# Second-half weights of eight mode groups read in 8 KB runs, and an uneven split by partitions moved to a later transfer

## The chip, the cores and the metric

The kernel runs on one core of a Trainium2 chip. That core has a matrix engine (TensorE, PE in the profile, with its weight loads as PEld), a vector engine (DVE), a scalar engine (ACT), GpSimd (POOL), a sync engine (SP), and sixteen DMA engines that all queues share. The metric is the device time of one execution in microseconds. Three unprofiled runs of the kernel before took 431.48, 431.50 and 431.73 us, so the median is 431.5 us. Lower is better.

## The reference

Sliding-window causal attention (batch 8, 8 heads, 576 positions, head dimension 64, window 64) is followed by a spectral mixing layer:

```
attn = softmax(q k^T / 8, masked to 0 <= i - j < 64) v        # 8 x 8 x 576 x 64
x    = attn, heads side by side                               # 8 x 576 x 512
X    = rfft(x, axis=1)[:, :64]                                # 64 modes
Yr   = Xr w_r - Xi w_i ;  Yi = Xr w_i + Xi w_r                # w_r, w_i: 64 x 512 x 512, one matrix a mode
y    = irfft(Y, 576)
u    = x + y
out  = u + max(u w_ch, 0)                                     # w_ch: 512 x 512
```

All inputs are float32 in HBM. The two weight tensors of the modes are 64 MB each, and each element is used once, for the eight batches; q, k and v are 9.4 MB each.

## The kernel before

**Work.** First comes the attention, in two halves of heads, then the 64 modes, then the inverse transform with the last product and the output. The weights of the modes are read all the while, from the first microseconds on. Every load of weights and of q, k and v is issued on POOL's queue, because it turns float32 into bfloat16 on its way, and the queue is served in the order of issue. A load of 1 MB as the profile counts it is 1 MB of bfloat16 in SBUF and 2 MB of float32 read.

**Modes in groups.** Modes are taken in groups of four, 16 groups in all, through the list `steps`. Groups 0 to 9 (`EARLY = 10`) are worked in two halves of the contracted channels: the first halves (`hb = 0`) during the attention, from heads 0 to 3; the second halves (`hb = 1`) after it. One step of a half takes two loads, one of `moe_w_r` (`ri = 0`) and one of `moe_w_i` (`ri = 1`), each with four modes. In it a partition holds two rows of 512 channels of each mode, so one contiguous run in HBM is 4 KB and lands as 2 KB. The last six groups come whole, two modes a load, with four rows on a partition: runs of 8 KB that land as 4 KB. In the text a load is named by its step, so (15, 0) is the `ri = 0` load of step 15, the second half of group 5.

**Products.** `mode_half` (L201) does the four modes of a half step: two products of 128 rows for each mode, every mode in its own 32 columns of the PE array, 8 matmuls of 512 columns a load. `mode_pair` (L215) does the whole modes, 16 matmuls of 256 columns a load. The left-hand side is the transform X with Xr, Xi and -Xi laid side by side: `XQ[0]` for heads 0 to 3, `XQ[1]` for heads 4 to 7, where partition p has channels 2p and 2p + 1. `whole_modes` (L675) re-lays the X of the last 24 modes so that partition p has channels 4p to 4p + 3 (`XA`, in the memory of `XQ[0]`), with eight small matmuls by a strided identity, four ACT copies and DVE negations; it stands before the third step of the second halves.

**Loading.** `load_weights` (L151) issues loads as buffers come free: eight of 1 MB in two rings (`ringA` with 3, `ringB` with 5). The last six groups use `ringA` alone. A buffer is free when PE has consumed it. POOL's DMAs take eight semaphores in turn, so that at most eight of them are under way and the ninth waits for the first to land.

**The uneven split.** One load, (15, 0) (`SPLIT`, L105), is cut: three modes in one DMA of 128 partitions, and the fourth mode in six DMAs over 87, 2, 4, 6, 5 and 24 partitions (`SHARES`, L106).

**Around it.** The loop at L1067 runs the second halves and the whole modes. For each load it calls the products, then `load_weights`, then a share of the other work (`advance`): products of x with `w_ch` (`x_jobs`, L655), which need the load of `w_ch` issued at L1096, and, near the end, the inverse transform of the modes that are done. After the last load come the last modes' products, the remaining tiles and the output.

```
            elif (at, ri) == SPLIT:
                parts = [[(p, p + 1, p + 2), (p + 3,)]]
...
            open_to = "a" if at >= 2 * EARLY else "aby" if at < EARLY + 2 else "ab"
...
            for size in SHARES if nload == UNEVEN and len(ps) == 1 else (128,):
```

Of the kernel before, what the change touches and what calls it, by code (L numbers as in the profile page):

```python
# [13 lines left out]
ALU = mybir.AluOpType  # L14
# [12 lines left out]
def kernel(  # L27
# [10 lines left out]
    nc = tc.nc  # L38
    B, H, S, D = q.shape
    NM = moe_w_r.shape[0]  # L40
    DM = moe_w_ch.shape[0]
# [7 lines left out]
    HALF = DM // 2  # L49
    NJ = 2  # L50
    NW = DM // 128
# [16 lines left out]
    ident_bf = consts.tile([128, 128], BF16, name="ident_bf")  # L68
# [14 lines left out]
    XQ = {0: xpool.tile([128, 3 * NJ + 2, B, NM], BF16, name="XQ0")}  # L83
# [14 lines left out]
    steps = [(grp, 0) for grp in range(EARLY)] + [(grp, 1) for grp in range(EARLY)]  # L98
# [2 lines left out]
    NMF = 4 * (NGRP - EARLY)  # L101
    XA = XA[:, 0:(3 * NW + 2) * B * NMF].rearrange("p (s b m) -> p s b m", b=B, m=NMF)
    steps += [(grp, hb) for grp in (*range(EARLY, LAST), *range(LAST + 2, NGRP), LAST, LAST + 1) for hb in range(2)]
    ONES = 3, 0
    SPLIT = EARLY + 5, 0  # L105
    SHARES = 87, 2, 4, 6, 5, 24  # L106
    wlist = []
    for at, (grp, hb) in enumerate(steps):
        for ri in range(2):
            p = 4 * grp  # L110
            if (at, ri) == ONES:
                parts = [[(p, p + 1)], [(p + 2,)], [(p + 3,)]]
            elif grp >= EARLY:
                p += 2 * hb
                parts = [[(p, p + 1)]]
            elif (at, ri) == SPLIT:
                parts = [[(p, p + 1, p + 2), (p + 3,)]]
# [5 lines left out]
    UNEVEN = wstart[SPLIT[0]] + SPLIT[1]  # L123
    assert sum(SHARES) == 128

    def lend(t, g=2):
        t = t.rearrange("p (t g j e) -> p t g j e", g=g, j=NJ, e=DM)
# [23 lines left out]
    def load_weights(n):  # L151
        nonlocal nload
        while nload < len(wlist):
            at, parts, hb, ri = wlist[nload]
            if 2 * n <= sum(len(ps) for ps in parts):
                return
            if nload in lent:
                w = lent[nload]
            else:
                open_to = "a" if at >= 2 * EARLY else "aby" if at < EARLY + 2 else "ab"  # L160
                h = min(open_to, key=lambda h: held[h][0] if len(held[h]) == room[h] else -1)
                if len(held[h]) == room[h]:
                    if held[h][0] not in spent:
                        return
                    held[h].pop(0)
                held[h].append(nload)
                if h == "y":
                    w = lentY
                else:
                    w = {"a": ringA, "b": ringB}[h].tile([128, 4, NJ, DM], BF16, name="wi" if ri else "wr", tag="wt")  # L170
            src = moe_w_i if ri else moe_w_r
            if at >= 2 * EARLY:
                w = w.rearrange("p (m h) j e -> p m (h j) e", m=2)
                p = parts[0][0]
                for m, k, lo, hi in ((0, 1, 0, NW), (1, 1, 0, NJ), (1, 1, NJ, NW)) if nload == len(wlist) - 1 else ((0, 2, 0, NW),):
                    nc.gpsimd.dma_start(  # L176
                        out=w[:, m:m + k, lo:hi],
                        in_=src[p + m:p + m + k].rearrange("m (p j) e -> p m j e", j=NW)[:, :, lo:hi])
# [3 lines left out]
                continue  # L182
            to = 0
            for ps in parts:
                row = 0
                for size in SHARES if nload == UNEVEN and len(ps) == 1 else (128,):
                    of = src[ps[0]:ps[-1] + 1, HALF * hb:HALF * hb + HALF, :].rearrange("g (p j) e -> p g j e", j=NJ)
                    nc.gpsimd.dma_start(out=w[row:row + size, to:to + len(ps)], in_=of[row:row + size])  # L188
                    row += size
# [8 lines left out]
    def spend(at, ri):  # L198
        spent.update(i for i, w in enumerate(wlist) if w[0] == at and w[3] == ri)

    def mode_half(psm, at, ri):  # L201
        grp, hb = steps[at]
        pairs = range(4 * grp, 4 * grp + 4)
        for j in range(NJ):
            for p in pairs:
                g = p % 4
                nc.tensor.matmul(out=psm[32 * g:32 * g + 32, :],  # L207
                                 lhsT=XQ[hb].rearrange("k s b m -> k (s b) m")[:, (3 * j + 1 - ri) * B:(3 * j + 5 - ri) * B, p],
                                 rhs=wtiles[p, hb, ri][:, j], start=(ri == 0 and j == 0), stop=(ri == 1 and j == NJ - 1),
                                 tile_position=(0, 32 * g))  # L210
        for p in pairs:
            wtiles.pop((p, hb, ri))
        spend(at, ri)

    def mode_pair(psm, at, ri):  # L215
# [17 lines left out]
    with tc.manual_schedule():  # L233
# [177 lines left out]
        at = scratch[:, 3 * NTC * NM:3 * NTC * NM + NTC]  # L411
# [6 lines left out]
        for nm in ("k", "q", "v"):  # L418
# [17 lines left out]
                         op0=ALU.max, op1=ALU.min)  # L436
# [82 lines left out]
        for it in range(-3, NU + 3):  # L519
# [23 lines left out]
            g = starts.get(it + 2)  # L543
# [26 lines left out]
        trigX = zpool.tile([128, 128], BF16, name="trigX")  # L570
        trigXr = zpool.tile([128, 128], FP32R, name="trigXr")
        XL = zpool.tile([128, 3 * NW + 2, B, 8], BF16, name="XL")
        trpool = pool("trpool", bufs=2, reuse_waits="tile")

        banks = {"m": pool("ps_mc", bufs=2, space=PSUM, reuse_waits="tile"),
# [5 lines left out]
        def bank(h, shape=(128, DM), dtype=FP32, name=None):  # L581
            return banks[h].tile(list(shape), dtype, name=name or "ps" + h, tag="bank")
# [482 lines left out]
        spread = []  # L1065
        n0, n1 = 2 * EARLY, 4 * (NGRP - EARLY)
        for i, (grp, hb) in enumerate(steps[EARLY:]):  # L1067
            if i == 2:
                whole_modes()
            if i == EARLY:  # L1070
                while tables:
                    tables.pop(0)()
                close(stmp2, yp, ringB)
                Zall = pool("zall", side="right").tile([2 * NM, B, DM], FP32R, name="Zall")
                x_jobs(pool("xp1", side="right", reuse_waits="tile"), NX0, NT)
                utpool = pool("utpool", side="right", reuse_waits="tile")
                nc.vector.memset(YT[:, :, :, rows], 0.0)
                homes.append(utpool.tile([128, 2, DM], FP32, name="utx"))
                spread = spread_steps(homes[0])
                given = 0  # L1080
            psm = bank("m")
            for ri in range(2):
                if half == n0 + n1 - 2:
                    while jobs or pend:
                        advance()
                (mode_half if grp < EARLY else mode_pair)(psm, EARLY + i, ri)
                load_weights(len(wlist))
                while ready:
                    ready.pop(0)()
# [101 lines left out]
```

## Time and profile before

| | |
|---|---|
| median of three runs | 431.5 us (431.48 to 431.73) |
| the profiled execution | 432.55 us |
| its span, first to last instruction | 430.4 us |
| PE busy | 327.7 us (76%) |
| DVE busy | 239.4 us (56%) |
| ACT busy | 182.4 us (42%) |
| POOL busy | 106.9 us (25%) |
| DMA | 93.28 MB as landed, 217 GB/s on average; 163.58 MB read from HBM |

The span is divided into engines' busy time, and the DMA share is the mean busy share of the sixteen DMA engines. Packets overlap a little, so the share can stand over 1. The chain that ended last follows the work back from the end of the execution; a piece of it named DMA is the time from the issue of a load to its landing, queueing included. The trace also holds, for each load, the sixteen times at which a DMA engine told that its part had landed; the last of them releases whoever waits.

### The profile page before, as it was taken

To read this page: it belongs to the slowest core of one execution; us is meant where nothing else is said; L and a number is where in the kernel's file an instruction comes from. 1 tells how busy PE (TensorE), PEld (TensorE's weight loads), DVE (VectorE), ACT (ScalarE), POOL (GpSimd) and SP (SyncE) were. 2 spreads that over 40 slices of the span, in tenths; PEclk is the share of its full clock that TensorE was granted. 3 is DMA by queue.
4 is the path that set the end of the run, shared out by engine and by line. 5 is a ranking of instruction groups with operands and counts; after the bars stand their busy time and mean duration, and the time that the engine had idled before them with its cause. 6 is when DMAs were issued, how large, how long until landed. Compare 5 with 4: busy or idle time off the path is not lost.

```text
span 430.4 us, 11427 instructions
## 1 busy us (share of the span) xinstructions
PE 327.7 (76%) x4962; PEld 219.4 (51%) x5006; DVE 239.4 (56%) x509; ACT 182.4 (42%) x330; POOL 106.9 (25%) x159
## 2 busy tenths in 40 slices
PE   6888899888999989975317246576586758989994
PEld 3666767576667666751104123344454545545552
DVE  8688787867676776876103212132222224874995
ACT  6665667565666657532201101124122213433663
POOL 8321223222132131112015100011111111120894
PEclk9999999999999999996556865579988889999999
DMA  8999999999999999999999999999999999996698
GB/s 205 212 211 212 211 212 211 211 212 211 212 211 211 212 213 210 213 211 213 211 257 173 211 212 212 215 214 215 215 215 214 214 214 214 215 215 123 226 368 305
DMA packets 40978, 93.28 MB, mean 217 GB/s; under 512 B 2688, under 2 KB 2944, under 8 KB 40928
## 3 DMA queue, kind: packets, MB, share of 16 engines
q0 software_dynamic: 35216, 81.80, 98.7%
q1 hardware_dynamic: 5568, 10.62, 6.8%
q8 instruction: 39, 0.64, 0.5%
q10 hardware_dynamic: 144, 0.13, 0.1%
q14 instruction: 11, 0.09, 0.1%
HBM read 163.58 MB, written 9.44 MB: 402 GB/s over the span
## 4 chain that ended last, share of the span: by engine, by line
DMA 55%; PE 25%; issue 11%; DVE 3%; POOL 3%; ACT 2%; DVEq 0%; POOLq 0%
DMA wi<-in_moe_w_i_dram 24%; DMA wr<-in_moe_w_r_dram 15%; DMA rawk<-in_k_dram 8%; DMA wch<-in_moe_w_ch_dram 8%; PE tr L269 4%; PE s L316 3%; PE s L328 2%; PE pt L336 2%; PE vb L281 2%; PE psm L207 2%; PE psz L655 2%; PE psm L225 1%; PE o L356 1%; PE s L308 1%; DMA vd<-in_k_dram 1%
## 5 line engine op out<-in xcount | busy, mean ns | idle before, releaser
L655 PE MATMUL psz<-wch,tr 128*128 128x512 f32 x176 | 62.8, 488 | 12.4 <-DMA wch<-in_moe_w_ch_dram 11.4
L876 DVE CAST xw<-psz 128x512 fp32r<-128x512 f32 x36 | 24.9, 692 | 80.1 <-PE psz L655 79.4
L320 DVE TENSOR_REDUCE mx<-s 128x4 fp32r<-128x512 f32 x72 | 49.6, 689 | 24.0 <-PE s L316 23.7
L623 ACT CAST tr<-ptx 128x512 fp32r<-128x512 bf16 x36 | 21.2, 590 | 90.3 <-PE ptx L648 90.3
L655 PEld LDWEIGHTS psz<-wch,tr 128*128 128x128 f32 x176 | 36.7, 232 | 20.2 <-issue 11.8
L330 ACT ACTIVATE p<-s 128x512 bf16<-128x512 f32 x72 | 39.7, 603 | 13.2 <-PE s L328 13.2
L207 PEld LDWEIGHTS <-XQ 128*32 128x32 bf16 x320 | 13.0, 175 | 43.7 <-issue 25.5
L316 PE MATMUL s<-kT,qT 64*64 64x128 bf16 (+1 forms) x576 | 29.1, 221 | 6.7 <-issue 6.7
L273 ACT COPY kT<-tr 128x576 bf16<-128x576 bf16 x32 | 23.2, 724 | 23.2 <-PE tr L269 23.2
L207 PE MATMUL psm<-wi,XQ 128*32 128x512 bf16 x144 | 15.1, 498 | 18.4 <-DMA wi<-in_moe_w_i_dram 18.4
L339 DVE COPY pts<-pt 128x1024 bf16<-128x1024 bf16 (+1 forms) x40 | 25.2, 630 | 5.3 <-PE pt L336 3.8
L273 ACT COPY qT<-tr 128x576 bf16<-128x576 bf16 x32 | 23.3, 728 | 9.6 <-PE tr L269 9.4
L316 PEld LDWEIGHTS <-qT 64*64 64x64 bf16 x576 | 18.0, 107 | 17.7 <-issue 17.2
L176 POOL DMA_DIRECT2D wr<-in_moe_w_r_dram x12 | 8.4, 697 | 74.4 <-PE psm L225 38.0
L328 PE MATMUL s<-mx,ident_r 128*128 128x512 f32 x72 | 26.2, 437 | 0.0
L695 DVE TENSOR_TENSOR stg<-psm,Yfour 128x512 bf16<-128x512 f32 x10 | 6.9, 691 | 34.3 <-PE psm L207 31.6
L207 PE MATMUL psm<-wr,XQ 128*32 128x512 bf16 x120 | 12.8, 509 | 16.0 <-DMA wr<-in_moe_w_r_dram 15.4
L273 ACT COPY vT<-tr 128x576 bf16<-128x576 bf16 x32 | 23.3, 727 | 4.0 <-PE tr L269 4.0
L225 PEld LDWEIGHTS <-XQ 128*32 128x32 bf16 x256 | 9.5, 151 | 29.1 <-issue 26.8
L188 POOL DMA_DIRECT2D wi<-in_moe_w_i_dram x18 | 13.6, 754 | 42.7 <-PE psm L207 31.9
L336 PE MATMUL pt<-ident_bf,p 128*128 128x128 bf16 x288 | 23.2, 220 | 0.7 <-issue 0.5
L256 POOL DMA_DIRECT2D rawk<-in_k_dram x15 | 8.1, 539 | 60.5 <-PE tr L269 49.5
(260 smaller groups left out, 678.6 us busy)
## 6 DMA issues: line engine op xcount, KB each, us to landing
wi<-in_moe_w_i_dram POOLq DMA_DIRECT2D x29, 1024.0 KB, 18.0
wr<-in_moe_w_r_dram POOLq DMA_DIRECT2D x26, 1024.0 KB, 17.3
out_dram<-ut SPq DMA_DIRECT2D x29, 256.0 KB, 2.7
rawv<-in_v_dram POOLq DMA_DIRECT2D x16, 288.0 KB, 16.4
rawk<-in_k_dram POOLq DMA_DIRECT2D x15, 288.0 KB, 15.2
rawq<-in_q_dram POOLq DMA_DIRECT2D x15, 288.0 KB, 15.1
x_sb<-in_moe_w_r_dram POOLq DMA_DIRECT2D x2, 1024.0 KB, 16.3
out_dram<-utx SPq DMA_DIRECT2D x6, 256.0 KB, 2.4
```

Of the source, the lines that this page charges most:

```text
L207: nc.tensor.matmul(out=psm[32 * g:32 * g + 32, :], lhsT=XQ[hb].rearrange("k s b m -> k (s b) m")[:, (3 * j + 1 - ri) * B:(3 * j + 5 - ri) ...
L269: nc.tensor.transpose(out=pt[ro, j, :], in_=raw[ro, TH * half + j, :], identity=ident_bf[ro, ro])
L273: nc.scalar.copy(out=to, in_=pt.rearrange("p j n -> p n j"))
L316: nc.tensor.matmul(out=s[ro, t, lo:128], lhsT=lq, rhs=kT[ro, 64 * n - 64 + lo:64 * n + 64], start=False, stop=True, skip_group_check=True)
L320: nc.vector.tensor_reduce(out=mx, in_=s, axis=AX.X, op=ALU.max, negate=True)
L328: nc.tensor.matmul(out=s, lhsT=ident_r, rhs=mx.unsqueeze(2).to_broadcast([128, 4, 128]), start=False, stop=True, skip_group_check=True)
L330: nc.scalar.activation(out=p[:, 4 * c2:4 * c2 + 4, :], in_=s, func=ACT_F.Exp, scale=EX_SCALE)
L336: nc.tensor.transpose(out=pt[:, t, :], in_=st[u]["p"][:, t, :], identity=ident_bf)
L339: nc.vector.tensor_copy(out=ps[:, 0:nt, :], in_=pt[:, 0:nt, :])
L623: nc.scalar.copy(out=tr, in_=pt)
L655: nc.tensor.matmul(out=pz, lhsT=tr[:, c, :], rhs=wch[:, c, :], start=(c == 0), stop=(c == NDCH - 1))
L876: nc.vector.tensor_copy(out=XW[i], in_=multiply(tr))
```

## The change

The second halves of groups 2 to 9 (`WIDE = 2`: steps 12 to 19, sixteen loads) are laid differently. Two modes share the 128 partitions: partition 2p takes four rows of the one mode, and partition 2p + 1 four rows of the other, in runs of 8 KB that land as 4 KB. One load is two DMAs of 512 KB, one for each pair of modes. A new function, `wide_modes`, makes an X to match (`XE`, in the memory of `XQ[1]`): for each of the two modes of a pair, X with zeros on the partitions of the other. `mode_wide` does 16 matmuls of 512 columns a load where `mode_half` does 8. `whole_modes` moves one step earlier, to the second step of the second halves, and its copy of `XL` moves behind `wide_modes`, which first uses the memory of `XL` for its strided identity.

Load (15, 0) is no longer split. In its place the first load of the last six groups, (20, 0), is cut into six DMAs: 25 partitions of both modes, 11 of both, then 80 of each mode by itself, then 12 of each.

```diff
+    XE = XQ[1].rearrange("p s b m -> p (s b m)")
+    WIDE = 2
+    NE = 2 * (EARLY - WIDE)
+    SHARES = 25, 11, 80, 12
+    XE = XE[:, 0:2 * (3 * NW + 2) * B * NE].rearrange("p (h s b m) -> p h s b m", h=2, b=B, m=NE)
-    SPLIT = EARLY + 5, 0
-    SHARES = 87, 2, 4, 6, 5, 24
...
             if at >= 2 * EARLY:
...
+                if nload == wstart[2 * EARLY]:
+                    row = 0
+                    for i, size in enumerate(SHARES):
+                        for m in [slice(0, 2)] if i < 2 else [slice(0, 1), slice(1, 2)]:
+                            nc.gpsimd.dma_start(
+                                out=w[row:row + size, m],
+                                in_=src[p:p + 2][m].rearrange("m (p j) e -> p m j e", j=NW)[row:row + size])
+                        row += size
...
+            if at >= EARLY + WIDE:
+                w = w.rearrange("p (q h) j e -> p q (h j e)", q=2)
+                for i in range(2):
+                    p = parts[0][2 * i]
+                    nc.gpsimd.dma_start(
+                        out=w[:, i], in_=src[p:p + 2, HALF:DM, :].rearrange("h (p j) e -> p h (j e)", j=NW))
+                    wtiles[p, hb, ri] = w[:, i].rearrange("p (j e) -> p j e", j=NW)
...
-                for size in SHARES if nload == UNEVEN and len(ps) == 1 else (128,):
...
+    def mode_wide(psm, at, ri):
+        grp, hb = steps[at]
+        for j in range(NW):
+            for g in range(4):
+                nc.tensor.matmul(out=psm[32 * g:32 * g + 32, :],
+                                 lhsT=XE[:, g % 2].rearrange("k s b m -> k (s b) m")[:, (3 * j + 1 - ri) * B:(3 * j + 5 - ri) * B,
+                                                                                    2 * (grp - WIDE) + g // 2],
+                                 rhs=wtiles[4 * grp + g - g % 2, hb, ri][:, j], start=(ri == 0 and j == 0),
+                                 stop=(ri == 1 and j == NW - 1), tile_position=(0, 32 * g))
...
+        def wide_modes():
+            nc.vector.memset(sprE, 0.0)
+            for r in range(2):
+                for h in range(2):
+                    nc.vector.tensor_copy(out=sprE[:, r, h, h::2], in_=ident_bf[:, r::2])
+            pts = [[bank("zt"[r == 0]) for j in range(NJ)] for r in range(2)]
+            for r in range(2):
+                for j in range(NJ):
+                    for h in range(2):
+                        nc.tensor.matmul(
+                            out=pts[r][j][:, 2 * B * NE * h:2 * B * NE * (h + 1)], lhsT=sprE[:, r, h],
+                            rhs=XQ[1][:, 3 * j + 1:3 * j + 3, :, 4 * WIDE:4 * EARLY].rearrange(
+                                "p t b (m h) -> p (t b) m h", h=2)[:, :, :, h],
+                            start=(h == 0), stop=True, skip_group_check=True)
+            nc.vector.memset(XE[:, :, 3 * NW:], 0.0)
+            for r in range(2):
+                for j in range(NJ):
+                    i = 3 * (NJ * r + j)
+                    px = pts[r][j].rearrange("p (h t b m) -> p h t b m", h=2, t=2, b=B)
+                    nc.scalar.copy(out=XE[:, :, i + 1:i + 3], in_=px)
+                    nc.vector.tensor_scalar(out=XE[:, :, i], in0=px[:, :, 1], scalar1=-1.0, scalar2=None, op0=ALU.mult)
...
-            if i == 2:
+            if i == WIDE - 1:
                 whole_modes()
+            if i == WIDE:
+                wide_modes()
...
-                (mode_half if grp < EARLY else mode_pair)(psm, EARLY + i, ri)
+                (mode_half if i < WIDE else mode_wide if grp < EARLY else mode_pair)(psm, EARLY + i, ri)
```

More of the change, by code (lines that the diff above doesn't have):

```diff
@@ L174, in load_weights @@
                 p = parts[0][0]
[L175 to L178, printed above, removed]
+                if nload == wstart[2 * EARLY]:
[6 more added lines that the diff above has]
+                        row += size
+                else:
+                    for m, k, lo, hi in ((0, 1, 0, NW), (1, 1, 0, NJ), (1, 1, NJ, NW)) if nload == len(wlist) - 1 else ((0, 2, 0, NW),):
+                        nc.gpsimd.dma_start(
+                            out=w[:, m:m + k, lo:hi],
+                            in_=src[p + m:p + m + k].rearrange("m (p j) e -> p m j e", j=NW)[:, :, lo:hi])
                 wtiles.update(((p + m, ri), w[:, m]) for m in range(2))
@@ L182, in load_weights @@
                 continue
+            if at >= EARLY + WIDE:
+                w = w.rearrange("p (q h) j e -> p q (h j e)", q=2)
+                for i in range(2):
+                    p = parts[0][2 * i]
+                    nc.gpsimd.dma_start(
+                        out=w[:, i], in_=src[p:p + 2, HALF:DM, :].rearrange("h (p j) e -> p h (j e)", j=NW))
+                    wtiles[p, hb, ri] = w[:, i].rearrange("p (j e) -> p j e", j=NW)
+                nload += 1
+                n -= 4
+                continue
             to = 0
             for ps in parts:
[L185 to L189 removed]
+                nc.gpsimd.dma_start(
+                    out=w[:, to:to + len(ps)],
+                    in_=src[ps[0]:ps[-1] + 1, HALF * hb:HALF * hb + HALF, :].rearrange("g (p j) e -> p g j e", j=NJ))
                 for i, p in enumerate(ps):
@@ L212, in mode_half @@
             wtiles.pop((p, hb, ri))
+        spend(at, ri)
+    def mode_wide(psm, at, ri):
[7 more added lines that the diff above has]
+                                 stop=(ri == 1 and j == NW - 1), tile_position=(0, 32 * g))
+        for i in range(2):
+            wtiles.pop((4 * grp + 2 * i, hb, ri))
         spend(at, ri)
```

6 lines of the change are left out of this document (2 added, 4 removed).

## The prediction

> **What bounds the kernel now.** I read the page first, then the busy time by stretches, the DMA issues, PE's order of time near the end, and the sixteen landings that the trace holds for each load. From the page:
>
> ```profile
> span 430.4 us, 11427 instructions
> ...
> DMA  8999999999999999999999999999999999996698
> ...
> q0 software_dynamic: 35216, 81.80, 98.7%
> ...
> q8 instruction: 39, 0.64, 0.5%
> ...
> DMA 55%; PE 25%; issue 11%; DVE 3%; POOL 3%; ACT 2%; DVEq 0%; POOLq 0%
> ```
>
> POOL's queue keeps the DMA engines busy until slice 36, at about 390 us; then comes a tail of compute. So the landing of the last load sets the end, if PE is ready for it. Stretches of ten microseconds give the price of the run length (the last two columns are DMA share and GB/s):
>
> ```profile
> 250.00:260.00 10.00, 4.44 (x30) 2.40 (x29) 1.38 (x2) 0.58 (x1) 0.00 (x0) 0.67 1.12 212
> 300.00:310.00 10.00, 6.71 (x69) 4.80 (x69) 3.88 (x6) 2.50 (x5) 1.40 (x2) 1.00 1.06 215
> ```
>
> The first is in runs of 4 KB, the second in runs of 8 KB. The landings give it finer. The first engine to land has 39.62 us for eight loads of 4 KB runs (235.76 to 275.38), 4.953 us each, and 88.12 us for eighteen of 8 KB runs (280.26 to 368.38), 4.896 each.
>
> The sixteen engines go at one rate but do not stand level. In (14, 1) they land between 219.14 and 224.88 us, a spread of 5.7 us; in the 4 KB stage they land 0, 0.1, 0.5, 0.5, 0.5, 0.8, 1.0, 1.8, 3.4, 3.6, 4.5, 4.5, 4.6, 4.7, 4.9 and 5.7 us after the first. Eight engines are late. The 39 fetches of instructions, 16 KB each, hold one engine for 0.89 to 1.05 us a time, and their durations repeat with a period of eight, so I read that eight engines take them in turn. A load is usable at its last landing, so the latest engine is what counts.
>
> PE's order of time near the end:
>
> ```profile
> 360.59 0.67 PE L225 MATMUL psm<-wr,XL 128*32 128x256 bf16 x16 [1.08 <-DMA wr<-in_moe_w_r_dram]
> ...
> 376.18 0.66 PE L225 MATMUL psm<-wi,XL 128*32 128x256 bf16 x16 [0.20 <-DMA wi<-in_moe_w_i_dram]
> ...
> 393.69 0.69 PE L225 MATMUL psm<-wr,XL 128*32 128x256 bf16 x16
> ...
> 394.73 0.66 PE L225 MATMUL psm<-wi,XL 128*32 128x256 bf16 x12
> 395.89 0.44 PE L225 MATMUL psm<-wi,XL 128*32 128x256 bf16 x4 [0.51 <-DMA wi<-in_moe_w_i_dram]
> ```
>
> PE waits 1.08 us for the load that lands at 360.55; from there it is nearly full, waits 0.20 for a load at 376, takes at 393.69 a load that landed at 390.87, and waits only 0.51 us for the last one. A DMA gain at the very end alone is worth 0.5 us; a larger one must already be there at 360.
>
> **The change part by part.** The sum is against the profiled execution, 432.55 us (span 430.4 and 2.15 around it); the median of 431.5 is 1.05 below it, and I take the same difference off.
>
> *Packets.* Sixteen loads go from 4.953 to 4.896 us: 16 x 0.057 = -0.91 us on every engine. Two DMAs for a load in place of one: the 512 KB load at 44.08 took 2.44 us of the queue, half of 4.95 and no more, so I take 0.
>
> *The old split goes.* Its rows:
>
> ```profile
> wch<-in_moe_w_ch_dram POOLq DMA_DIRECT2D x1, 1024.0 KB, 32.6
> ...
> wr<-in_moe_w_r_dram POOLq DMA_DIRECT2D x1, 768.0 KB, 35.1
> ...
> wr<-in_moe_w_r_dram POOLq DMA_DIRECT2D x1, 174.0 KB, 31.3
> ```
>
> From the last landing of (14, 1), 224.88, to that of (15, 1), 237.54, pass 12.66 us. In between are w_ch, which takes the first engine 2.53 us (219.14 to 221.68), and two loads: 2.53 + 2 x 4.953 = 12.44. The split thus cost the latest engine 0.22 us instead of saving it time: each of the small pieces lands 0.16 to 0.18 us after the one before even where an engine has nothing of it. -0.22.
>
> *The new split.* The landings tell how rows are dealt. After the piece of 87 rows nearly all engines are 0.93 to 1.0 us later, six rows at 0.154 us; the latest is 0.56 later, three rows; so rows go out in order, ceil(rows/16) to an engine, and the latest engine is the fifteenth of sixteen. By that rule 25, 11, 80, 80, 12, 12 give engines 1 to 11 two rows of 8 KB more than an even deal (0.306 us each: +0.61 us), the twelfth none, the thirteenth 4 fewer, and the last three 6 fewer: -1.84 us, less four empty pieces at 0.17 each: -1.2. The series of short semaphore writes, by length, put the late eight at engines 8 to 15. So the latest engine gains 1.2, and late engines 8 to 11, of which the best placed stands 1.1 us behind the latest, lose 0.6. At the end of before, the latest has also taken a fetch (at 373.8); in the new order an engine of the other group is last, with its own fetch (0.95): -1.1 + 0.6 = -0.5 at the last landing. At 360, where the latest of before has not yet had that fetch and the other group has, it is -1.1 + 0.6 + 0.95 = +0.45. Bounds: -1.2, if the group were not pushed; +0.95, if the latest engine were not relieved and another fetch hit it.
>
> *PE.* `mode_wide` issues 16 matmuls where there were 8. Rows:
>
> ```profile
> 272.26 1.11 PE L207 MATMUL psm<-wr,XQ 128*32 128x512 bf16 x8 [3.91 <-DMA wr<-in_moe_w_r_dram]
> ...
> 277.20 1.11 PE L207 MATMUL psm<-wi,XQ 128*32 128x512 bf16 x8 [1.26 <-DMA wi<-in_moe_w_i_dram]
> ...
> 278.63 0.70 POOL L176 DMA_DIRECT2D wr<-in_moe_w_r_dram  x1 [29.05 <-PE psm L207]
> ```
>
> +1.11 us a load at the granted clock of 0.5 (+0.7 at full clock, by 0.68 for eight at 237.59), under waits of 1.3 to 4.0 us for loads. It costs nothing by itself. If the cover went, the third load of the last six groups (278.63) would be issued later, and it is the first that finds only three buffers. The latest engine then still has work until 286.9; a load issued to a dry engine starts about 2.4 us later (228.40 to 235.76 less 4.95). With 1.1 us earlier landings PE may be about 4.5 us late there before an engine runs dry. I take 0.
>
> *New X.* `whole_modes` is moved one step up: eight matmuls 0.8 us, four ACT copies 1.7, DVE 1.7. `wide_modes` adds eight matmuls (0.8 by the same rows), four ACT copies of 512 columns (0.58 by L712: 2.3), on DVE two memsets (0.2 to 0.4 each), four small copies (0.15 to 0.4), four negations (0.36 for 192 columns, so 0.5 each, estimated): about 3.5 us. PE waits 2.30 us before 200.11 and 3.58 before 205.12, which takes it in; XE may be ready about 201 to 203. Without that cover up to 3 us of PE move to the stall for w_ch (11.36 us of PE waiting until 227.83). 0.
>
> *POOL, queues, fetches.* POOL issues 15 DMAs more at 0.5 to 0.75 us, from a POOL that is busy 1 to 2 us in 10. With eight under way, half-size loads keep 19.6 us in the queue, against a spread of 5.7; the six pieces leave at least 6 us for the latest engine. w_ch is issued later, behind such waits, but its place in the queue, and so its landing, stay. SP has nothing in this stage. About 300 more instructions are one more fetch (11427/39 = 293 each): 0, and +0.95 at worst if it meets the last engine.
>
> **Sum.** At 360: -0.91 - 0.22 + 0.45 = -0.68. PE's row from 360.59 moves by it, and by the 0.20 of waiting at 376: its last twelve matmuls end at 395.39 - 0.88 = 394.5. The last landing is 395.85 - 0.91 - 0.22 - 0.5 = 394.2. So the last four start at 394.5 in place of 395.89: -1.4, and the 34.5 us behind them stay. 432.55 - 1.4 = 431.15; on the median scale 430.1. With a tenth for pieces that cost a little more: 430.2. What is late next is PE, not the DMA.
>
> **A rule against a row.** The 87-row landings speak for the ceil rule. The Trainium skill, page "DMA: Bandwidth & Descriptors", section "Why a DMA increments its semaphore by 16 and not by 1", says that a DMA runs on the largest number of engines up to 16 that divides its slowest dimension, and names the ceil deal as an exception for some direct copies; the trace shows the exception. By its main rule the new split is another one, worked out as the second rival.
>
> **The rivals.** A measurement tells about 0.2% (0.86 us) from no change.
>
> 1. *Hidden by PE.* The engines that are pushed are late at 360 by all that the packets and the old split gained, so nothing is earlier there; only the 0.5 us of PE's last wait is won: 431.0. For it: PE takes the 390.87 load 2.8 us late. Against: the pieces have enough data to hide their ends.
>
> 2. *Dealt by divisors.* 25 rows would go to five engines, 11 to eleven, 12 to twelve: five engines get 22 rows of 8 KB in place of 16, +1.84 us. If a late engine is among them, landings at 360 are -1.13 - 1.1 + 1.84 + 0.95 = +0.56, and the end about 431.6; if the latest itself is, up to 432.3. Against: the landings of 87 rows.
>
> 3. *Slower: PE late at the change of rings.* If matmuls and the stall for w_ch leave PE over 4.5 us late at the third whole load, all engines run dry, and each microsecond beyond is one at the end. PE's work from 200 to 282 us would be 16 x 2.2 + 10 x 2.7 for the jobs + 3 + 11.4 of stall = 77 of 82 us at half clock; it is close only if the clock stays low (before, it was 0.79 in the catching-up at 230 to 240). 7 us late: 430.1 + 2.5 = 432.6; 8 us late, 433.6. It ends slower than before from about 6 us on. For it: PE doubles its work there, and runs in order.
>
> **How the numbers follow.** The forecast 0.52 (430.2, own range 429.4 to 430.64); hidden 0.24 and dealt by divisors 0.07, both within 0.2%; slower 0.17. The forecast's cases are faster by over 0.2%: 0.52; same 0.31; slower 0.17. From 429.4, with all gains and no push, to 432.4, which leaves out most of the third rival, is 0.82.
>
> **What would show it.** 212 GB/s should turn to 214 or 215 from 200 to 277 us, with a DMA share of 1.06; the packets over 2 KB rise by some 4100. The last landing before the whole modes should be near 276.0 (277.16 before), the load now at 360.55 near 359.9, the last near 394.2 with a spread of about 5 us, not 2.9. PE should not wait before its last four matmuls. It is wrong if the third load of the last groups is issued after 283 us, if 8 KB runs alternating between two modes go no faster than 212 GB/s, or if PE's row from 360 grows.

## The result, and the profile after

The changed kernel takes 430.84 us (median of 20 executions, 430.52 to 431.68), the kernel before, measured beside it, 431.65 us: ratio 0.9983, 95% interval 0.9977 to 0.9990, 0.8 us or 0.17% less. A later comparison gave 0.9973 (0.9960 to 0.9987). The forecast was 430.2 us. Ratios here leave out one execution, of p4_newsplit below, that took 541.19 us where its other nine took 430.77 to 431.88.

The page of the changed kernel, the span, the row of the DMA engines, the queues and the share of the span in the chain that ended last:

```profile
span 429.0 us, 11775 instructions
...
DMA  8999999999999999999999999999999999995797
...
q0 software_dynamic: 31424, 81.80, 97.7%
...
q8 instruction: 40, 0.66, 0.6%
...
q14 instruction: 12, 0.10, 0.1%
...
DMA 54%; PE 30%; DVE 6%; issue 6%; ACT 2%; POOL 1%; DVEq 0%; POOLq 0%
```

The same bytes go in 31424 packets, 3792 fewer. There are 348 more instructions (304 in a second profile of the same kernel), 316 of them PE's matmuls and weight loads, and one more fetch of 16 KB on q8. The chain still runs through DMA for 54% of the span. By stretches (busy time of PE, PEld, DVE, ACT and POOL, then clock, DMA share, GB/s):

```profile
250.00:260.00 10.00, 6.82 (x46) 3.36 (x45) 1.38 (x2) 0.59 (x1) 2.36 (x5) 0.67 1.07 215
300.00:310.00 10.00, 5.31 (x60) 3.90 (x61) 3.19 (x5) 1.76 (x3) 1.43 (x2) 0.98 1.06 214
```

The first stretch is now like the second: DMA share 1.07 for 1.12, 215 GB/s for 212. PE is half as busy again there, under its waits. PE's order of time near the end:

```profile
359.21 0.67 PE L254 MATMUL psm<-wr,XL 128*32 128x256 bf16 x16 [0.94 <-DMA wr<-in_moe_w_r_dram]
...
392.26 0.68 PE L254 MATMUL psm<-wr,XL 128*32 128x256 bf16 x16
393.30 0.87 PE L254 MATMUL psm<-wi,XL 128*32 128x256 bf16 x16
```

The load that PE took at 360.59 it now takes at 359.21. The row behind it has moved as a whole by 1.4 us, and the gap of 0.51 us before the last four matmuls is gone: the last engine lands at 393.69 (395.85 before), when PE is just there. The last mode matmul starts at 393.90, 2.16 us earlier than before (396.06). Yet the span is only 1.4 us shorter (428.98 against 430.37), since the stretch behind that matmul grew from 34.31 to 35.09 us. DVE's order of time at the end shows where, first of the kernel before:

```profile
424.09 0.68 DVE L986 TENSOR_TENSOR ut<-psy,x_sb 128x512 f32<-128x512 f32 x1
424.87 1.35 DVE L1055 SCALAR_TENSOR_TENSOR ut<-psz,ut 128x512 f32<-128x512 f32 x3
```

and of the changed kernel:

```profile
421.91 0.68 DVE L1038 TENSOR_TENSOR ut<-psy,x_sb 128x512 f32<-128x512 f32 x1
423.06 1.35 DVE L1107 SCALAR_TENSOR_TENSOR ut<-psz,ut 128x512 f32<-128x512 f32 x3 [0.47 <-PE psz L1049]
```

DVE idles 0.47 us ahead of its last three instructions, where it idled 0.10 before (424.77 to 424.87). The wait is put down to PE, but PE's last matmul starts 1.09 us before DVE's last but one instruction in the kernel before and 1.47 in the changed one, so PE is not what is late. Of the 0.78 us of growth, 0.37 are in this wait and 0.1 between DVE's last instructions and the last landing of the output. The rest, 0.31 us, lies between that landing and the end (1.04 and 1.35 us).

### The profile page after: what moved, and what is told of

It is laid out like the page before. It is cut to its first block, busy times and chain, and to the rows that moved or that the text cites. A ratio compares the mean times of both kernels' runs of the same rounds, so it can differ in the third digit from the quotient of the medians.

```text
span 429.0 us, 11775 instructions
## 1 busy us (share of the span) xinstructions
PE 349.6 (81%) x5142; PEld 226.7 (53%) x5142; DVE 241.6 (56%) x519; ACT 184.7 (43%) x334; POOL 113.5 (26%) x174
## 3 DMA queue, kind: packets, MB, share of 16 engines
q0 software_dynamic: 31424, 81.80, 97.7%
## 4 chain that ended last, share of the span: by engine, by line
DMA 54%; PE 30%; DVE 6%; issue 6%; ACT 2%; POOL 1%; DVEq 0%; POOLq 0%
DMA wr<-in_moe_w_r_dram 23%; DMA wi<-in_moe_w_i_dram 18%; DMA rawk<-in_k_dram 11%; PE tr L298 4%; PE s L345 3%; PE s L357 2%; PE s L337 2%; PE psz L685 2%; PE pt L365 2%; PE vb L310 2%; PE o L385 2%; PE psm L254 2%; DVE xw L874 2%; PE psm L223 1%; DVE XQ L893 1%
## 5 line engine op out<-in xcount | busy, mean ns | idle before, releaser
L685 PE MATMUL psz<-wch,tr 128*128 128x512 f32 x176 | 60.8, 476 | 11.3 <-DMA wch<-in_moe_w_ch_dram 10.0
L685 PEld LDWEIGHTS psz<-wch,tr 128*128 128x128 f32 x176 | 35.3, 223 | 18.9 <-issue 10.4
L337 PE MATMUL s<-mask_t,ident_bf 128*128 128x512 bf16 x72 | 28.4, 395 | 0.6
L235 PEld LDWEIGHTS <-XQ 128*32 128x32 bf16 x256 | 11.9, 147 | 31.8 <-issue 25.3
L254 PEld LDWEIGHTS <-XQ 128*32 128x32 bf16 x256 | 9.6, 151 | 28.8 <-issue 28.6
L184 POOL DMA_DIRECT2D wi<-in_moe_w_i_dram x14 | 9.5, 684 | 50.7 <-PE psm L254 29.8
L397 DVE TENSOR_TENSOR x_sb<-o,r 128x512 bf16<-128x512 f32 x32 | 22.1, 691 | 1.1
```

The lines of the kernel that those rows point to most:

```text
L235: nc.tensor.matmul(out=psm[32 * g:32 * g + 32, :], lhsT=XE[:, g % 2].rearrange("k s b m -> k (s b) m")[:, (3 * j + 1 - ri) * B:(3 * j + 5 ...
L337: nc.tensor.matmul(out=s, lhsT=ident_bf, rhs=mask_t[:, mk], start=True, stop=True)
L397: nc.vector.tensor_tensor(out=xo.rearrange("p c (h d) -> p c h d", d=64), in0=ov[:, :, :, 0:64], in1=rb, op=ALU.mult)
L685: nc.tensor.matmul(out=pz, lhsT=tr[:, c, :], rhs=wch[:, c, :], start=(c == 0), stop=(c == NDCH - 1))
```

## The experiments

The theory after the result: DMA gains of the forecast's kind move the row from 360 on, and the ten DVE instructions that `wide_modes` adds give part of it back at the end. The rivals: that the packets do all, the split nothing (or the reverse); that PE's doubled products cost something; that the longer end has another cause. All ratios are to the kernel before on the same chip; 0.001 is 0.43 us. Times in the table are from one profiled execution of each. "Load at 360" is the last landing of the load that PE took at 360.59 in the kernel before; "stretch" is from the start of the last mode matmul to the end of the span.

| kernel | ratio (95%) | load at 360 | last mode matmul | stretch |
|---|---|---|---|---|
| before | 1 | 360.55 | 396.06 | 34.31 |
| before_again | – | 361.34 | 395.94 | 34.29 |
| p4_nosplit | 0.9993 (0.9984–1.0002) | 360.51 | 395.35 | 34.32 |
| p4_newsplit | 0.9983 (0.9973–0.9992) | 360.29 | 395.10 | 34.32 |
| p8_nosplit | 0.9999 (0.9991–1.0008) | 360.11 | 395.07 | 35.11 |
| changed kernel | 0.9983 (0.9977–0.9990) | 359.16 | 393.90 | 35.09 |
| after_again (the same) | 0.9973 (0.9960–0.9987) | 359.53 | 394.43 | 35.08 |
| after_lean | 0.9972 (0.9960–0.9983) | 359.58 | 394.38 | 34.61 |
| lean_again (the same) | 0.9963 (0.9950–0.9976) | 359.21 | 393.77 | 34.31 |
| lean_nosplit | 0.9990 (0.9974–1.0005) | 360.57 | 395.09 | 34.29 |
| before_dve10 | 1.0012 (1.0003–1.0021) | 360.75 | 395.34 | 35.11 |
| before_act10 | 0.9990 (0.9976–1.0004) | 359.87 | 394.77 | 34.65 |
| before_pe2 | 1.0010 (0.9994–1.0026) | 361.10 | 395.71 | 34.65 |

**before_again**, the kernel before without an edit.

> The kernel before, unchanged, profiled once more. Its profiled execution took 432.55 us, 0.9 above its median of 431.65, so part of the 1.4 us between the two spans may be of that one execution. If the gain is as I summed it, the last landing is again near 395.9 us and PE's last matmuls of the modes again wait for it. If the execution was the odd one, its landings come 0.5 to 1 us earlier, or its tail is shorter.

It took 432.38 us in one execution, and its last load landed at 395.73, so the first profile was not the odd one. Together with before_dve10 and before_act10, whose loads are the same, it shows how far a landing wanders from one profile (and chip) to another: the load at 360 lands between 359.87 and 361.34. A difference of a few tenths in one profile of each is therefore no evidence; the ratios, of many executions, are.

**The splits and the packets, one at a time.** p4_nosplit is the kernel before without its split:

```diff
-            elif (at, ri) == SPLIT:
+            elif False:
...
-    UNEVEN = wstart[SPLIT[0]] + SPLIT[1]
+    UNEVEN = -1
```

> The kernel before without the uneven split: load (15, 0) is one DMA of 128 partitions. My theory: the old split cost the latest engine 0.22 us, so this is 0.2 to 0.4 us faster than before, with the spread of landings staying near 5.7 us after 230 us. Rival (the old split helped, and moving it is a loss that the packets pay for): 0.5 us or more slower.

p4_newsplit has beside that the new split of the first whole load (`SHARES = 25, 11, 80, 12` and the loop over it), with 4 KB runs:

> The kernel before with only the split changed: (15, 0) whole, (20, 0) cut into 25, 11, 80, 12; all runs stay at 4 KB. My theory: the new split relieves the late engines by about 1.2 us but PE is late next, so 0.3 to 0.6 us faster than before. Rival (the split is the whole gain): 0.8 us faster, as the changed kernel is. Rival (the split does nothing): as p4_nosplit.

p8_nosplit is the changed kernel without any split:

```diff
-                if nload == wstart[2 * EARLY]:
+                if nload == -1:
```

> The changed kernel with (20, 0) in one DMA: runs of 8 KB alone. My theory: 16 x 0.057 us and the 0.22 of the old split, less a fetch that meets the latest engine before 360 us: 0.4 to 0.8 us faster than before, 0.1 to 0.4 slower than the changed kernel. Rival (packets are the whole gain): 0.8 us faster, equal to the changed kernel. Rival (the split is the whole gain): equal to before.

The old split may have cost the 0.22 us that the prediction read from its landings: 0.9993 without it, an interval that takes in both 0 and 0.7 us. The new split alone gave 0.9983, the ratio that the whole change had in its first comparison and more than the 0.3 to 0.6 us expected, and the 8 KB runs alone gave 0.9999, nothing. Both are nearer to the rival that the split is the whole gain than to what was expected. The orders of time of PE, of p4_nosplit, of p4_newsplit and of p8_nosplit:

```profile
360.55 0.67 PE L225 MATMUL psm<-wr,XL 128*32 128x256 bf16 x16 [0.54 <-DMA wr<-in_moe_w_r_dram]
```

```profile
360.33 0.67 PE L234 MATMUL psm<-wr,XL 128*32 128x256 bf16 x16 [0.95 <-DMA wr<-in_moe_w_r_dram]
```

```profile
360.15 0.66 PE L254 MATMUL psm<-wr,XL 128*32 128x256 bf16 x16 [1.43 <-DMA wr<-in_moe_w_r_dram]
```

In p8_nosplit PE has this load 0.4 us earlier than in p4_nosplit, and the stretch behind is 0.8 us longer: in these two profiles that accounts for the lack of any gain. Where the packets' gain went shows in the landings. From (11, 1) to (19, 1) the first engine takes (270.92 - 189.11 - 2.53)/16 = 4.955 us a load in p4_nosplit, and (270.28 - 189.09 - 2.55)/16 = 4.915 in p8_nosplit (2.5 us is w_ch): 0.04 a load, 0.64 in all. The latest engine lands (19, 1) at 276.12 and at 276.40, so there the gain is gone altogether. p8_nosplit fetches instructions once more, and three of its fetches lie between 200 and 280 us (at 230.2, 245.2 and 274.4) where p4_nosplit has two; over the one at 274.4 the last landing's step to the next half load is 3.09 us, after 2.42 for the one before. In p4_nosplit the fetch at 274.8 leaves the last landing's step to (19, 1) at 4.95 us, a whole load's usual time. The queues of the two pages, p4_nosplit first:

```profile
q8 instruction: 39, 0.64, 0.5%
```

```profile
q8 instruction: 40, 0.66, 0.6%
```

**p2_nosplit** is p4_nosplit with runs of 2 KB, in two DMAs a load:

```diff
-                    nc.gpsimd.dma_start(out=w[row:row + size, to:to + len(ps)], in_=of[row:row + size])
+                    for j in [slice(0, 1), slice(1, 2)] if at >= EARLY + 2 and size == 128 and len(ps) == 4 else [slice(0, 2)]:
+                        nc.gpsimd.dma_start(out=w[row:row + size, to:to + len(ps), j], in_=of[row:row + size, :, j])
```

> The kernel before without any split, with the second halves of groups 2 to 9 in runs of 2 KB (each load in two DMAs, one for each of the two rows of a partition). Same output. It is the packet term of the sum, turned round. The first engine took 4.955 us a load in 4 KB runs and 4.915 in 8 KB runs. Theory of a fixed cost for each packet (32 more packets of an engine a load from 8 to 4 KB cost 0.04 us; 64 more from 4 to 2 KB then cost about 0.08): 5.03 to 5.05 us a load, last landing before the whole modes some 1.3 us later than without a split at 4 KB (276.12), time about 433. Rival (the price of a packet rises below 4 KB, because the landed run of 1 KB is too short): over 5.2 us a load, last landing after 280, time over 436.

The first engine took (273.27 - 189.38 - 2.53)/16 = 5.085 us a load: 0.13 more than at 4 KB for 33 more packets of an engine (43504 on q0 where p4_nosplit has 35056, over 16 loads and 16 engines), where the step from 8 to 4 KB costs 0.04 for 15 (p8_nosplit has 31216). The expectation had about twice as many of both, so its sum stands. That is nearer to a fixed cost for each packet than to the rival, but above the 5.03 to 5.05 expected. The stretches, of p2_nosplit and of p8_nosplit:

```profile
250.00:260.00 10.00, 4.87 (x29) 2.45 (x28) 1.37 (x2) 0.42 (x2) 2.96 (x4) 0.59 1.24 206
300.00:310.00 10.00, 8.41 (x76) 5.59 (x75) 2.99 (x5) 3.67 (x8) 1.02 (x2) 0.75 1.04 206
```

```profile
300.00:310.00 10.00, 5.68 (x62) 3.98 (x61) 3.19 (x5) 1.76 (x3) 1.41 (x2) 1.00 1.06 213
```

The whole took 440.38 us in one execution, far more than the landings explain: from 300 to 310 us this execution had a granted clock of 0.75 where p8_nosplit has 1.00, PE fell behind the loads, and the end came from PE. Why the clock was low in it, one execution doesn't tell, so only its rate is used.

**before_pe2**, PE's share of the change alone. Every product of the second halves of groups 2 to 9 is issued twice, so the values of these groups come out doubled:

```diff
                 g = p % 4
-                nc.tensor.matmul(out=psm[32 * g:32 * g + 32, :],
+                for twice in range(2 if at >= EARLY + 2 else 1):
+                  nc.tensor.matmul(out=psm[32 * g:32 * g + 32, :],
```

> The kernel before, with every product of mode_half issued twice in the second halves of groups 2 to 9 (16 matmuls of 512 columns a load in place of 8), 4 KB runs and the old split kept. The values of these groups come out doubled; no other work changes. It is PE's share of the change alone. Theory (hidden under PE's waits for loads, no engine runs dry at the third whole load): the third whole load is still issued before 280 us, the last landing is within 0.3 us of the kernel before, ratio 0.999 to 1.001; some 256 more instructions are about one more 16 KB fetch, which costs up to 0.95 us if it holds the latest DMA engine after 200 us, ratio then 1.001 to 1.002. Rival (PE late at the change of rings): the third whole load is issued after 283 us, ratio over 1.003.

PE's order of time, and POOL's, near the change of rings:

```profile
271.92 1.97 PE L208 MATMUL psm<-wr,XQ 128*32 128x512 bf16 x16 [3.88 <-DMA wr<-in_moe_w_r_dram]
277.67 1.12 PE L208 MATMUL psm<-wi,XQ 128*32 128x512 bf16 x16 [1.33 <-DMA wi<-in_moe_w_i_dram]
```

```profile
279.12 0.70 POOL L176 DMA_DIRECT2D wr<-in_moe_w_r_dram  x1 [29.03 <-PE ptx L649]
```

Sixteen matmuls took 1.1 to 2.0 us and PE still waited 1.3 to 3.9 us for loads; the third whole load was issued at 279.12 (278.63 before), so the slower rival did not come. The ratio of 1.0010 has an interval that holds both nothing and the 0.95 us of a fetch; this kernel too has 40 fetches on q8, three of them between 200 and 280 us. In the changed kernel itself the third whole load goes out at 278.29:

```profile
278.29 0.73 POOL L184 DMA_DIRECT2D wr<-in_moe_w_r_dram  x1 [3.50 <-PE psm L235]
```

**The longer end.** Two kernels turn the suspected cause on and off. before_dve10 adds ten small instructions to DVE in the kernel before:

```diff
+            for i in range(10):
+                nc.vector.memset(XL[:, i], 0.0)
             nc.vector.tensor_copy(out=XL, in_=XA[:, :, :, lo:lo + 8])
```

> The kernel before, with ten VectorE memsets of 64 columns added at the end of whole_modes, on columns of XL that the next instruction overwrites. Same output. Theory of VectorE's instruction stream: the stretch from the last mode matmul to the end grows from 34.3 to about 35.1 us although nothing else changes, ratio 1.0010 to 1.0025. Rival: ten memsets of some 0.1 to 0.2 us each at about 205 us are hidden, the stretch stays at 34.3 us and the ratio is 1.000.

before_act10 adds them to ACT instead, `nc.scalar.copy(out=XL[:, i], in_=XA[:, i, :, lo:lo + 8])`:

> The kernel before, with ten copies of 64 columns on ScalarE at the end of whole_modes, into columns of XL that VectorE overwrites next. Same output. It is the run with ten memsets on VectorE, with the ten instructions on another engine. Theory (VectorE's wait before its last instructions belongs to VectorE's own stream): no such wait (0.1 us idle or less before the last three), the stretch after the last mode matmul is 34.3 to 34.65 us. The 0.3 us between the last output landing and the end (1.04 us in the kernel before, 1.35 in all kernels with more instructions on any engine) tells whether any added instruction brings it: 1.35 if so, 1.04 if only streams of VectorE or PE matter. Rival (any ten more instructions bring the whole growth): 35.1 us.

after_lean takes the ten off DVE in the changed kernel:

```diff
         def wide_modes():
-            nc.vector.memset(sprE, 0.0)
...
-                    nc.vector.tensor_copy(out=sprE[:, r, h, h::2], in_=ident_bf[:, r::2])
+                    nc.scalar.copy(out=sprE[:, r, h, h::2], in_=ident_bf[:, r::2])
...
-            nc.vector.memset(XE[:, :, 3 * NW:], 0.0)
+            nc.scalar.mul(out=XE[:, :, 3 * NW:], in_=pts[0][0].rearrange("p (h t b m) -> p h t b m", h=2, t=2, b=B), mul=0.0)
...
-                    nc.vector.tensor_scalar(out=XE[:, :, i], in0=px[:, :, 1], scalar1=-1.0, scalar2=None, op0=ALU.mult)
+                    nc.scalar.mul(out=XE[:, :, i], in_=px[:, :, 1], mul=-1.0)
...
             if i == WIDE - 1:
                 whole_modes()
+                nc.gpsimd.memset(sprE, 0.0)
```

> The changed kernel, with the ten VectorE instructions that wide_modes adds given to other engines: the memset of the strided identity to GpSimd one step earlier, the four small copies, the zeros of XE (a product by 0 from PSUM) and the four negations to ScalarE. Same output. In the changed kernel the stretch from the last mode matmul to the end of the span is 35.09 us, in the kernel before 34.31; it is long in both kernels that hold wide_modes and short in all that do not. Theory (VectorE's longer instruction stream moves one of its instruction loads into the final chain): the stretch goes back to 34.3 us, and the time to 0.8 us below the changed kernel, about 430.0, ratio to before 0.9962 to 0.9970. Rival (the tail is longer because the last modes are earlier against other work, or by the streams of PE or POOL): the stretch stays at 35.1 us and the ratio at 0.998.

The groups of DVE at the end (busy time, mean of one, idle time before), of before_dve10, of before_act10 and of after_lean:

```profile
L1057 DVE SCALAR_TENSOR_TENSOR ut<-psz,ut 128x256 f32<-128x256 f32 (+1 forms) x3 | 1.4, 506 | 0.5 <-PE psz L999 0.5
```

```profile
L1057 DVE SCALAR_TENSOR_TENSOR ut<-psz,ut 128x256 f32<-128x256 f32 (+1 forms) x3 | 1.4, 507 | 0.1
```

```profile
L1106 DVE SCALAR_TENSOR_TENSOR ut<-psz,ut 128x256 f32<-128x256 f32 (+1 forms) x3 | 1.4, 505 | 0.1
```

Ten instructions on DVE at 201 us bring the wait of 0.5 us at 424 us, and a ratio of 1.0012; the same number on ACT does not bring it; taken off DVE, it goes. The wait belongs to DVE's own stream of instructions. That it is the loading of this stream is the likely reading, and the traces bear it out. In all four profiles with the wait (the changed kernel's two, p8_nosplit, before_dve10) the instruction that waits is DVE's 576th of 583 as the trace counts them, waits on semaphores included, and a transfer of 8 KB of instructions on queue q14 starts 1.42 to 1.46 us behind its start. In the nine without it (p2_nosplit aside) DVE has 570 to 573 instructions, and no transfer on q14 starts within 3.8 us behind the same instruction. The page rows of q14 show the one transfer more: 12 or 13 in the four, 11 in all others. That DVE waited for its instructions is still an inference, for this transfer starts only after the wait has ended. The Trainium skill, page "Runtime: NRT & Kernel Launch", section "Instruction fetch mechanics", says that an engine's instructions come in blocks of 256 and that crossing from one to the next is mostly hidden. The transfer here has 8 KB, where a fetch on q8 has 16; if the wait is such a crossing, about 0.37 us of it (0.47 less the usual 0.10) was not hidden here.

after_lean's first comparison did not hold the changed kernel, so the two were run side by side, with a third kernel that leaves the split out of after_lean.

> The changed kernel, unchanged, beside the two variants of it that follow. Every theory expects ratio 0.998 to 0.9985, the stretch from the last mode matmul to the end 35.1 us, and VectorE waiting some 0.47 us before its last but one instructions.

> The changed kernel with the ten added VectorE instructions given to ScalarE and GpSimd, once more, now beside the changed kernel. Of the 0.78 us by which the stretch after the last mode matmul grew, this variant gave back 0.48 before (34.61 us). Theory (the wait of VectorE is worth its length): ratio 0.001 below that of the changed kernel, about 0.997, time about 0.45 us less. Rival (what is won there is lost again in landings, since the first run of this variant had its last mode matmul 0.48 us later than the changed kernel): the same ratio as the changed kernel within 0.0005.

> The same variant without any split: the 8 KB runs alone, without the ten VectorE instructions. The 8 KB runs with them gave 0.9999. Theory (the gain of the packets, 0.4 us at the load that PE takes at 360, was eaten by the longer tail): the tail is 34.6 us, ratio 0.9985 to 0.999. Rival (the runs of 8 KB are worth nothing, their gain goes into one more instruction fetch on the latest DMA engine): ratio 0.9995 to 1.000.

In lean_again after_lean took 430.43 us (429.75 to 431.11), in after_again the changed kernel 430.88 (429.98 to 431.75), 0.45 us apart in the median, with ratios 0.9963 and 0.9973, as the theory of DVE's stream has it. The intervals overlap, so the ratios alone don't prove it; the wait in the trace and the 1.0012 of before_dve10 say the same. Among the kernels run after_lean is the fastest, and its interval, 0.9950 to 0.9976, lies wholly below 1.

The 0.31 us at the very end need not be the change's: after_lean has 1.35 us from the last output landing to the end in its first profile and 1.05 in its second. So the stretch varies by 0.3 from profile to profile. All four profiles with DVE's wait showed the long form, and three of nine without it (p2_nosplit with its low clock aside); whether the wait makes it likelier is open.

lean_nosplit gave 0.9990, in another comparison than p8_nosplit's 0.9999; the 0.0009 between them is again about the worth of DVE's ten instructions. It is the 0.9985 to 0.999 expected, but its stretch of 34.29 us is the short one, and its interval holds the rival's 1.000 too. Against p4_nosplit (0.9993) it makes the 8 KB runs worth 0.1 us, far within the uncertainty. Against lean_again in the same comparison the split is worth 0.0027, 1.2 us; between p8_nosplit and the changed kernel, of two comparisons, it was 0.0016, 0.7 us; at 4 KB, in one, 0.0010, 0.4 us. The sizes scatter as widely as the intervals, but all have one sign.

## Why the prediction was right, and where its terms were not

The direction held, and 430.84 us lies in the stated 429.4 to 432.4, though 0.2 us above the forecast case's own range (up to 430.64), and nearer to the first rival's 431.0 than to 430.2. The path held too (landings before 360, then PE's row). The gain was 0.8 us in one comparison, just inside the 0.2% that the prediction counts as no change, and 0.95 in the other (430.88 against 431.83), where 1.3 to 1.4 was forecast. The step that failed is the deal of rows in the new split, and with it the +0.45 at 360. By step:

- **The price of the packets** (-0.91) was too large. It came from comparing 4 KB loads of one stage with 8 KB loads of another, 0.057 a load; in the same stage it is 0.04, so -0.64 on the first engine. On the latest engine nothing of it was left without a split.
- **The fetch** was put at 0, with +0.95 "at worst if it meets the last engine". In the changed kernel one meets it: over the fetch at 274.8 the last landing's step to the end of (19, 1) is 3.40 us for half a load, after 2.41 for the half before, and the last landing there is 276.86, not 276.0. But the kernel before has a fetch at 276.0 as well, and one fetch more does not decide whether the latest engine is met: in p4_newsplit, which has none more, the step to (19, 1) is 5.68 us after 4.91, and in after_lean, which has one more, it is 2.52 after 2.42. The term belonged in the sum as a chance.
- **The old split's cost** (-0.22) agrees with p4_nosplit, as far as its interval tells.
- **The new split, relief.** From the end of (19, 1) to that of (20, 1) the last landing takes 8.65 us in the changed kernel and 8.42 to 9.17 in the other four profiles with this split, against 9.46 to 9.83 in the three without any. That is 0.3 to 1.4 us less, for the forecast 1.2. The four small pieces (25, 11, 12 and 12 rows) moved the last landing of the changed kernel by 0.19 to 0.31 us each.
- **The new split, deal of rows.** Here the mechanism was wrong. The forecast dealt the piece of 25 rows two to an engine, which would be 1.2 us on each of twelve engines. In the order of landing, which is clearest in lean_again, five engines are 2.88 to 3.02 us later after this piece, and the other eleven 0.16 to 0.67. Five rows of two modes are 10 x 0.306 = 3.06 us, so the 25 rows went to five engines; the landings of the other four profiles read the same way. So the deal of the second rival came for this piece, although the 87 rows of the old split were dealt by ceil. The rival's price did not come, because the five are early engines each time. In the four profiles with 8 KB runs all eight late engines are only 0.16 to 0.28 us later after the piece, the price of a piece without data. Over (20, 0) and (20, 1) the late eight take 8.96 to 9.18 us on average, where the 8 KB kernels without a split take 9.8. So no late engine was pushed, and the net +0.45 at 360 failed with its premise. The load at 360 lands at 359.16 to 359.58 in these four profiles, against 360.11 and 360.57 in the two with 8 KB runs and no split: about -1.0. Most of the change's gain is the split's, and the forecast had it down as a loss there. The spread fell from 6.5 us to about 4 also because the first engines ran dry: the first landing's step from the last piece to (20, 1), which was issued at 274.02, is 6.39 us where a load takes 4.9.
- **Sum at 360**: forecast -0.68, measured -1.38 in the profiles, with the wandering of 0.7 either way. The packets gave less than forecast and the split more.
- **PE's row** moved as a whole, as stated, and met the last landing within 0.1 us: landing at 393.69 with a spread of 3.7 us, predicted 394.2 and about 5. The last four matmuls follow without a gap. The first rival (hidden by PE) falls by the load at 360, although its time is the nearer one: in the four profiles this load is earlier than in any with the loads of before (359.87 to 361.34).
- **New X**: XE was ready later than the 201 to 203 worked out. PE waited 2.68 us at 201.11 and 1.68 at 204.67, and caught up at 212:

```profile
201.11 1.03 PE L730 MATMUL pst<-XQ,XL 128*128 128x256 bf16 x4 [2.68 <-DVE XL L725]
...
204.67 2.06 PE L235 MATMUL psm<-wr,XQ 128*32 128x512 bf16 x16 [1.68 <-DVE XQ L741]
...
212.02 0.44 PE L235 MATMUL psm<-wi,XQ 128*32 128x512 bf16 x2 [0.65 <-DMA wi<-in_moe_w_i_dram]
...
226.91 1.62 PE L685 MATMUL psz<-wch,tr 128*128 128x512 f32 x3 [10.01 <-DMA wch<-in_moe_w_ch_dram]
```

  The stall for w_ch shrank from 11.36 to 10.01 us, so the cover held, and 0 was right.
- **"The 34.5 us behind them stay"** failed: +0.78 in the profiles. Of this 0.46 goes with DVE's wait (35.09 us, where kernels without the wait but with the long end have 34.61 to 34.65), brought by the ten instructions that the forecast had costed only where they run. Without them, in lean_again, the gain is 1.4 us (430.43 against 431.83), the size of the forecast.
- **The scale.** The forecast took 1.05 off its sum because the profiled execution of the kernel before was slower than its median by that. The changed kernel's profiled execution, 430.76 us, stands at its median, and profile against profile the change is -1.8. One profiled execution is not a steady distance from the median. The spans agree with the forecast by luck: the last mode matmul moved by -2.16 us where the last four were forecast to move by -1.4, the stretch behind it grew by 0.78 where 0 was forecast, and together that is again -1.4.

## What to carry to other kernels

A load is usable when the latest DMA engine has landed, so a faster rate counts only as far as that engine has it: compare last landings, and put an instruction fetch that meets the latest engine into the sum as a chance (it moved the last landing by 0.7 to 1.2 us in p8_nosplit, p4_newsplit, the changed kernel and lean_nosplit). Read from the landings how the rows of each piece of a DMA were dealt: one piece's deal did not hold for another. Instructions added to one engine can cost at the far end of its stream; look at the gaps before its last instructions, and give helper work to an engine whose last instructions are not in the final chain. Where two profiles of one kernel put the same landing 0.7 us either side, separate the parts of a change by ratios of many executions, each part alone.

## What the runs showed of the hardware that was not expected

- Ten short DVE instructions at 201 us bring a 0.47 us gap on DVE at about 424 us; ten on ACT do not. In every profile with the gap, an 8 KB transfer of instructions starts some 1.45 us behind its end.
- A piece of 87 rows was dealt to nearly all engines, six rows each, but a piece of 25 rows to five engines, five rows each: 3.0 us on these, about 0.2 us on an engine that gets nothing.
- The split of a DMA into 25, 11, 80 and 12 rows relieved the last landing by some 0.3 to 1.4 us (8.42 to 9.17 us over two loads, 9.46 to 9.83 without).
- Runs of 2, 4 and 8 KB cost the first engine 5.085, 4.955 and 4.915 us for 1 MB as landed: the second halving of the packets gains a third of the first.
- From the last output landing to the end, 1.05 or 1.35 us pass, both in one and the same kernel.
